# The second exchange of a spectral layer: a read fetches what one back step wrote, into a quarter of the partitions

## The chip, the cores and the metric

The kernel runs on one core of a Trainium2 chip. Its time is the device time of one execution in microseconds (us); before the change the median of three executions was 1404.33 us (1404.03 to 1405.24). The engines are named as in the profile: PE is TensorE (PEld its weight loads), DVE is VectorE, ACT is ScalarE, POOL is GpSimd, SP is SyncE, which computes nothing and issues transfers. SPq and ACTq are the instruction queues of SP and ScalarE where they issue a transfer.

## The reference, cut to what matters

Input x is 2,048 rows of 512 numbers. Four layers follow each other, each added to x: spectral, attention, spectral, attention.

```python
def _A_ref(x, w_r, w_i):                      # spectral layer
    X = jnp.fft.rfft2(x.astype(jnp.float32), axes=(-2, -1))
    X = X * (w_r + 1j * w_i)
    return jnp.fft.irfft2(X, s=(S, D), axes=(-2, -1)).astype(jnp.bfloat16)

x = x + _A_ref(_layernorm(x), A_w_r, A_w_i)
x = x + _B_ref(_layernorm(x), B_wq, B_wk, B_wv, B_wo)   # attention, 32 heads, one shared key and value head
x = x + _A_ref(_layernorm(x), A_w_r, A_w_i)
x = x + _B_ref(_layernorm(x), B_wq, B_wk, B_wv, B_wo)
```

The change touches the spectral layer alone, which runs twice. In the text "layer 0" and "layer 1" are its two runs.

## The kernel before, in words

The two-dimensional Fourier transform is done with matmuls. A transform over the 2,048 rows is split in two factors, 16 and 128, and between the factors the data has to change its layout over the partitions. This is done through DRAM: a tile is written out and read back with another arrangement. There is one such exchange on the way forward (tiles A1, D1, A2; the profile calls the SBUF tiles A and the DRAM tile D) and a second one on the way back (B1, D2, B2; the profile calls them B and D). The 256 frequencies are handled as two halves, h = 0 and 1, of 128 complex frequencies, so a row of one half is 256 numbers, 512 bytes in bf16.

The steps of a layer:

- `forward` and `first` turn rows into frequencies and do the 128-point factor. Each `first` writes two of the 16 row groups t to D1 (line 281). `cross1(g, h)` (line 284) reads a quarter of D1 back into 32 partitions of A2: `A2[32 * g:32 * g + 32, h, :, :]`.
- `filtered(j)`, j = 0 to 7: the half is h = j // 4, and b4 = 4 * (j % 4) says which four of the 16 values of b it handles. It does the 16-point factor (TensorE, line 213 in helper `rotate`), evicts (ScalarE, line 330), and multiplies by the weights (VectorE, lines 334 to 347).
- `back(j)`: the 16-point factor in the other direction, for the same four b, two at a time. Each two are evicted to B1 (line 358, once line 356) and then written to D2 (line 359): two writes of 128 KB for each `back`.
- `cross2(h, g, eng)` (line 362): reads four of the 16 t of half h into all 128 partitions of B2. Each of these reads needs all of b, so all four `back` steps of the half.
- `along(q, h)` (line 384): the 128-point factor, matmuls with table CS over the partitions of B2 for two of the 16 t, evicted to AT (lines 387 and 389).
- `last(t, h)` (lines 396 to 399): the transform back along a row, accumulated over both halves in one PSUM bank.

Four engines, PE, ACT, DVE and SP, run these steps in the order in which the program issues them (a manual schedule). The string STEPS writes out the order of the middle part: f is `filtered`, b is `back`, j empties the list of products, and x is the second exchange of half 0, all four reads of it, issued on SP after `b3`. The four reads of half 1 come later, behind all of half 0's `along`, two on SP and two on ScalarE's queue. Then come the loads of wq and wo (layer 0), the first four `last`, and the loop over half 1.

Waits are by semaphore, and an engine that waits holds up everything behind it in its queue. For SP that means that a read waiting for the landing of a write holds up every later write.

Half 0's `along` begins right after the last `back`; half 1's `along` follows the four early `last` steps.

Of the kernel before, what the change touches and what calls it, by code (L numbers as in the profile page):

```python
# [11 lines left out]
P = 128  # L12
BF = mybir.dt.bfloat16
# [32 lines left out]
VCELLS = 128  # L46
LASTW = 6
NEGATE = 7
STEPS = "f0 f1 f2 b0 f3 b1 b2 j3 b3 x0 f4 f5 f6 b4 f7 b5 j7 b6 b7"
NORMED, NORMG = (1,), ((3,), (3,), (3,))  # L50
OUTK, LATE_AT = 2, 4
TWICE = ((7,), 8)
# [23 lines left out]
def host_tables():  # L76
    import ml_dtypes
    bf = lambda a: np.ascontiguousarray(np.asarray(a, dtype=np.float32).astype(ml_dtypes.bfloat16))
    tabs = {}
    p = np.arange(P, dtype=np.float64)  # L80
    m = np.arange(P, dtype=np.float64)
    t16 = np.arange(16, dtype=np.float64)

    row = (128 * np.arange(4)[None, :, None] + np.arange(P)[:, None, None]).astype(np.float64)
    ff = (np.arange(256)[None, None, :] + 1).astype(np.float64)

    half = 2 * np.pi * np.arange(256) / 512.0
    cos, sin = np.cos(half), np.sin(half)
    cos[128], sin[0] = 0.0, 0.0
    cos[129:], sin[129:] = -cos[1:128][::-1], sin[1:128][::-1]  # L90
    turn = (row * ff).astype(np.int64) % 512
    c, s = np.concatenate([cos, -cos])[turn], -np.concatenate([sin, -sin])[turn]
    tabs["PH"] = bf(np.concatenate([c[..., :128], s[..., :128], c[..., 128:], s[..., 128:]], axis=2))

    ang = 2 * np.pi * (16 * p[:, None, None] + t16[None, :, None]) * m[None, None, :] / 2048.0
    tabs["C1"], tabs["S1"] = bf(np.cos(ang)), bf(np.sin(ang))

    ti, ai = np.divmod(np.arange(P), 8)
    same = (ai[:, None] == ai[None, :]).astype(np.float64)
    ang = 2 * np.pi * ti[:, None] * ti[None, :] / 16.0  # L100
    tabs["G"] = bf(np.stack([same * np.cos(ang), same * np.sin(ang), -same * np.sin(ang)], axis=1))

    b16 = np.arange(16, dtype=np.float64)
    mm = 16 * ai[None, None, :] + b16[None, :, None]
    ang = 2 * np.pi * (ti[:, None, None] * ti[None, None, :] / 16.0 + ti[None, None, :] * mm / 2048.0)
    tabs["H1"] = bf(same[:, None, :] * np.cos(ang))
    tabs["H2"] = bf(same[:, None, :] * np.sin(ang))

    ang = 2 * np.pi * m[:, None] * p[None, :] / 128.0
    tabs["CS"] = bf(np.stack([np.concatenate([np.cos(ang), np.sin(ang)], axis=1),  # L110
                              np.concatenate([-np.sin(ang), np.cos(ang)], axis=1)], axis=1))

    frow = (128 * np.arange(2)[None, :, None] + np.arange(P)[:, None, None] + 1).astype(np.float64)
    dd = np.arange(512)[None, None, :].astype(np.float64)
    ang = 2 * np.pi * frow * dd / 512.0
    cf = np.where(frow == 256, 1.0, 2.0) / (S * D)
    tabs["PSC"] = bf(cf * np.cos(ang))
    tabs["PSS"] = bf(-cf * np.sin(ang))
    tabs["ident"] = bf(np.eye(P, dtype=np.float32))
    tabs["hmask"] = (np.arange(P)[:, None] // DH % 2 == np.arange(2)[None, :]).astype(np.float32)  # L120
    return tabs


class Tables:


    def __init__(self, nc):
        self.nc, self.host, self.dram = nc, host_tables(), {}
# [82 lines left out]
def rotate(nc, ps, c, s, sn, re_im, first):  # L211

    nc.tensor.matmul(ps, lhsT=c, rhs=re_im, start=True, stop=False, skip_group_check=True)  # L213
    nc.tensor.matmul(ps[:, 0:128], lhsT=s, rhs=re_im[:, 128:256], start=False, stop=False, skip_group_check=True)
    nc.tensor.matmul(ps[:, 128:256], lhsT=sn, rhs=re_im[:, 0:128], start=False, stop=True, skip_group_check=True)  # L215


def spectral_layer(nc, tc, tabs, ht, A_w_r, A_w_i, x_sb, bigp, pre, norm, att, feed, weights):
    C1, S1, S1N, PH, ident = (tabs[n] for n in ("C1", "S1", "S1N", "PH", "ident"))
    with tc.tile_pool(name="workA", bufs=2) as work, tc.tile_pool(name="tabA", bufs=1) as tabA, \  # L220
# [32 lines left out]
            weights(k)  # L253

        D1 = dram.tile([2, 16, P, 256], BF, name="D1")
        D2 = dram.tile([2, P, 16, 256], BF, name="D2")
        turned = len(feed.xT)
        xT = feed.xT[0] if turned else bigp.tile([P, NC, 16, P], BF, name="xT", tag="big")
        Pk, A1, A2 = big("Pk"), big("A1"), big("A2")
# [58 lines left out]
        Z, B1, B2 = big("Z"), big("B1"), big("B2")  # L318
        M = big("M").rearrange("p h t c -> p (h t c)").rearrange("p (i j b r f) -> p i j b r f", i=2, j=4, b=4, r=2)

        def filtered(j):

            h, b4 = j // 4, 4 * (j % 4)
            hf = slice(128 * h, 128 * h + 128)
            X = work.tile([P, 4, 2, 128], BF, name="X", tag="X", bufs=3)
            for b in range(b4, b4 + 4, 2):
                ps = bank()
                for i in range(2):
                    rotate(nc, ps[:, i, :], G[:, 0, :], G[:, 1, :], G[:, 2, :], A2[:, h, b + i, :], i == 0)
                nc.scalar.copy(out=X[:, b - b4:b - b4 + 2, :, :], in_=ps.rearrange("p j (r f) -> p j r f", r=2))  # L330
            m1, m2 = (M[:, i, j % 4] for i in range(2))
            wrb = wr_sb[:, b4:b4 + 4, hf].unsqueeze(2).to_broadcast([P, 4, 2, 128])
            wib = wi_sb[:, b4:b4 + 4, hf].unsqueeze(2).to_broadcast([P, 4, 2, 128])
            nc.vector.tensor_tensor(out=m1, in0=X, in1=wrb, op=ALU.mult)
            joined()
            nc.vector.tensor_tensor(out=m2, in0=X, in1=wib, op=ALU.mult)
            products.append((j, m1, m2))
# [3 lines left out]
        def joined():  # L341

            while products:
                j, m1, m2 = products.pop()
                Zv = Z[:, j // 4, 4 * (j % 4):4 * (j % 4) + 4, :].rearrange("p b (r f) -> p b r f", r=2)
                nc.vector.tensor_tensor(out=Zv[:, :, 0, :], in0=m1[:, :, 0, :], in1=m2[:, :, 1, :], op=ALU.subtract)
                nc.vector.tensor_tensor(out=Zv[:, :, 1, :], in0=m1[:, :, 1, :], in1=m2[:, :, 0, :], op=ALU.add)  # L347

        def back(j):
            h, b4 = j // 4, 4 * (j % 4)  # L350
            for b in range(b4, b4 + 4, 2):
                ps = bank()
                for i in range(2):
                    rotate(nc, ps[:, i, :], H1[:, b + i, :], H2N[:, b + i, :], H2[:, b + i, :], Z[:, h, b + i, :], i == 0)
                if j == 7 and b > b4:
                    nc.vector.tensor_copy(out=B1[:, h, b:b + 2, :], in_=ps)
                else:
                    nc.scalar.copy(out=B1[:, h, b:b + 2, :], in_=ps)
                nc.sync.dma_start(out=D2[h, :, b:b + 2, :], in_=B1[:, h, b:b + 2, :])

        def cross2(h, g, eng):
            eng.dma_start(out=B2[:, h, 4 * g:4 * g + 4, :],
                          in_=D2[h].rearrange("(t a) b c -> t (a b) c", t=16)[4 * g:4 * g + 4].rearrange("t m c -> m t c"))

        for step in STEPS.split():
            j = int(step[1])
            if step[0] == "f":
                filtered(j)
            elif step[0] == "b":
                back(j)  # L370
            elif step[0] == "j":
                joined()
            else:
                for g in range(4):
                    cross2(0, g, nc.sync)

        AT = big("AT").rearrange("p h t c -> p (h t c)").rearrange("p (t h c) -> p t h c", t=16, h=2)

        def along(q, h, use_scalar):

            ps = bank()
            for i in range(2):
                for j in range(2):
                    nc.tensor.matmul(ps[:, i, :], lhsT=B2[:, h, 2 * q + i, 128 * j:128 * j + 128], rhs=CS[:, j, :],
                                     start=(j == 0), stop=(j == 1), skip_group_check=True)
            if use_scalar:
                nc.scalar.copy(out=AT[:, 2 * q:2 * q + 2, h, :], in_=ps)
            else:
                nc.vector.tensor_copy(out=AT[:, 2 * q:2 * q + 2, h, :], in_=ps)
# [10 lines left out]

        for q in range(8):
            along(q, 0, q % 2 == 0)
        for g in range(4):
            cross2(1, g, (nc.sync, nc.scalar)[g % 2])
        weights(20)
        early = 4
        for t in range(early):
# [2 lines left out]
        for q in range(9):  # L410
# [9 lines left out]
            g, odd = divmod(q - 3, 2)  # L420
# [746 lines left out]
def full_kernel(ctx, tc, A_x, A_w_r, A_w_i, B_x, B_wq, B_wk, B_wv, B_wo, out):  # L1167
# [63 lines left out]
    for layer in range(2):  # L1231
        norm_in, norm_out = make_norm(), make_norm()
        spectral_layer(nc, tc, tabs, ht, A_w_r, A_w_i, x_sb, bigp, norm, norm_in, att, feed,
                       weights if layer == 0 else lambda k: None)
        feed = attention_layer(nc, tc, att, norm_in, norm_out, x_sb, wo_sb, None if layer == 0 else store)
        norm = norm_out
# [47 lines left out]
```

## Time and profile before

| | us |
|---|---|
| median of three executions | 1404.33 |
| the profiled execution, its own time | 1406.89 |
| its span, first to last instruction | 1405.1 |
| granted TensorE clock over the span | 0.999 |
| spectral layer 1, first `forward` to last `last`, about | 708 to 788 |
| wait of TensorE before half 1's `along`, layer 0 | 1.87 |
| the same, layer 1 | 0.85 |

The page gives busy times and shares for each engine, the DMA queues, the chain of work that ended last, and the costliest groups of instructions by line. A timeline row has start, length, engine, line, operation and tiles, and in brackets the idle time ahead of it with what ended it. For a DMA the length in a queue's timeline is the time to issue it, and the DMA view gives the time from issue to landing; landing times in the text are the sum of the two. The text calls the eight reads of the second exchange x0 to x7 and the two writes of `back(j)` wja and wjb.

### The profile page before, as it was taken

How to read it: one execution, taken by the hardware profiler on the slowest of the kernel's cores; microseconds unless marked ns; L12 is line 12 of the kernel's file. 1: busy time of each engine (PE TensorE's matmuls, PEld its weight loads, DVE VectorE, ACT ScalarE, POOL GpSimd, SP SyncE). 2: the span in 40 equal slices, each digit the busy share in tenths (PEclk: the TensorE clock that was granted, in tenths of full speed). 3: DMA queues.
4: the chain of work that ended last, by engine and by line, in shares of the span. 5: the costliest groups of instructions: out<-in, count | busy, mean ns of one | idle time of the engine just before them, and what ended most of it. 6: DMA issues, size and time to landing. Idle time of an engine off the chain costs nothing.

```text
span 1405.1 us, 34816 instructions
## 1 busy us (share of the span) xinstructions
PE 1341.5 (95%) x14050; PEld 470.6 (33%) x14118; DVE 1310.0 (93%) x2271; ACT 1330.8 (95%) x1542; POOL 822.7 (59%) x479
## 2 busy tenths in 40 slices
PE   8799999999999999999997999999999999999998
PEld 6553232223222222222275422322222222222222
DVE  5679999999999999999966899999999999999997
ACT  6579999999999999999966899999999999999997
POOL 1125676667666667666700267666666666666664
PEclk9999999999999999999999999999999999999999
DMA  8710000000000000001074000000000000000000
GB/s 251 201 38 2 1 2 2 2 1 2 2 2 1 2 2 1 2 1 35 13 199 133 2 2 2 2 2 9 5 6 1 6 9 5 2 2 9 9 2 16
DMA packets 45682, 34.52 MB, mean 25 GB/s; under 512 B 10064, under 2 KB 43088, under 8 KB 45008
## 3 DMA queue, kind: packets, MB, share of 16 engines
q1 hardware_dynamic: 43120, 31.08, 7.8%
q8 instruction: 110, 1.80, 0.5%
q10 hardware_dynamic: 2400, 1.21, 0.3%
q14 instruction: 52, 0.43, 0.1%
HBM read 20.22 MB, written 10.49 MB: 22 GB/s over the span
## 4 chain that ended last, share of the span: by engine, by line
ACT 48%; PE 33%; issue 9%; DVE 7%; DMA 3%; SPq 0%; POOL 0%; DVEq 0%; ACTq 0%
ACT e L1082 47%; PE pv L871 13%; PE sc L916 10%; DVE ph L956 3%; PE aux L916 2%; PE ps L266 2%; DVE ln_stats L156 1%; PE aux L455 1%; PE ps L213 1%; DMA B<-D 1%; DVE ph L988 1%; PE pv L886 1%; PE aux L684 1%; DMA x_sb<-in_A_x_dram 0%; DMA D<-B 0%
## 5 line engine op out<-in xcount | busy, mean ns | idle before, releaser
L1082 ACT ACTIVATE e<-sc 128x1024 bf16<-128x1024 f32 x1328 | 1218.1, 1167 | 2.9 <-PE sc L916 2.9
L980 POOL TENSOR_TENSOR ph<-ph,step 128x1024 int32<-128x1024 int32 x404 | 762.8, 1891 | 413.1 <-DVE ph L988 292.7
L956 DVE TENSOR_SCALAR ph<-aux 128x512 uint16<-128x512 f32 x1440 | 903.8, 678 | 20.5 <-PE aux L916 15.9
L871 PE MATMUL pv<-ph,vaug 128*32 128x512 bf16 x4320 | 548.8, 386 | 0.6 <-POOL ph L980 0.3
L916 PE MATMUL sc<-QT,Kv 32*128 32x512 bf16 x2656 | 521.8, 380 | 23.5 <-ACT e L1082 16.3
L871 PE MATMUL pv<-e,vaug 128*32 128x512 bf16 x2656 | 484.0, 384 | 0.3 <-ACT e L1082 0.3
L916 PE MATMUL aux<-QT,Kv 32*128 32x512 bf16 x1440 | 455.8, 384 | 1.0 <-DVE ph L956 0.5
L916 PEld LDWEIGHTS <-Kv 32*128 32x128 bf16 x4096 | 183.4, 91 | 525.9 <-issue 517.5
L886 PE MATMUL pv<-wo_sb,zeros 128*32 128x512 bf16 x1200 | 257.8, 383 | 0.0
L871 PEld LDWEIGHTS <-vaug 128*32 128x32 bf16 x6976 | 147.5, 94 | 292.6 <-issue 281.6
L988 DVE TENSOR_SCALAR ph<-ph 128x2048 uint16<-128x2048 uint16 x316 | 216.4, 685 | 0.5
L162 POOL TENSOR_TENSOR ln_rstd<-ln_veps,mhalf 128x4 f32<-128x4 f32 x16 | 16.5, 1033 | 120.6 <-DVE ln_veps L161 120.5
L156 DVE BATCH_NORM_STATS2 ln_stats<-x_sb 128x6 f32<-128x512 bf16 x64 | 43.5, 679 | 22.9 <-ACT x_sb L418 17.0
L886 PEld LDWEIGHTS <-zeros 128*32 128x32 bf16 x1200 | 60.1, 94 | 1.9 <-issue 0.3
L786 DVE STREAM_TRANSPOSE oT<-pv 128x512 f32<-128x512 f32 x64 | 45.2, 706 | 9.2 <-PE pv L871 9.2
L185 ACT ACTIVATE Pk<-ps,ln_rstd 128x256 bf16<-128x256 f32 x64 | 26.8, 472 | 19.7 <-PE ps L266 15.2
L266 PE MATMUL ps<-tab_PH,xT 128*128 128x256 bf16 x256 | 35.3, 286 | 1.6 <-DVE oT L786 0.8
L280 DVE CAST A<-ps 128x512 bf16<-128x512 f32 x28 | 19.3, 689 | 18.3 <-PE ps L215 18.3
L455 PE MATMUL aux<-xTa,wq_sb 128*128 128x512 bf16 x90 | 32.6, 384 | 2.8 <-issue 2.4
L808 POOL TENSOR_TENSOR on<-oT,rden 128x512 bf16<-128x512 f32 x30 | 31.7, 1056 | 2.0 <-DVE rden L812 1.8
L684 PE MATMUL aux<-wo_sb,ph 128*128 128x512 bf16 x72 | 26.1, 383 | 3.6 <-issue 2.1
L213 PE MATMUL ps<-Z,tab_H 128*128 128x256 bf16 x64 | 15.1, 275 | 13.0 <-DVE Z L347 12.9
(108 smaller groups left out, 669.7 us busy)
## 6 DMA issues: line engine op xcount, KB each, us to landing
D<-A SPq DMA_DIRECT2D x32, 128.0 KB, 2.9
A<-D SPq DMA_DIRECT2D x16, 256.0 KB, 3.5
D<-B SPq DMA_DIRECT2D x32, 128.0 KB, 2.4
B<-D SPq DMA_DIRECT2D x12, 256.0 KB, 4.0
wr_sb<-in_A_w_r_dram SPq DMA_DIRECT2D x2, 1024.0 KB, 6.2
wi_sb<-in_A_w_i_dram SPq DMA_DIRECT2D x2, 1024.0 KB, 8.5
tab_H<-const_H SPq DMA_DIRECT2D x4, 512.0 KB, 6.8
out_dram<-x_sb SPq DMA_DIRECT2D x15, 128.0 KB, 1.7
```

The lines of the kernel that those rows point to most:

```text
L156: nc.vector.bn_stats(st, src)
L266: nc.tensor.matmul(ps[:, j, :], lhsT=xT[:, cc, 2 * k + j, :], rhs=PH[:, cc, 256 * h:256 * h + 256], start=(cc == 0), stop=(cc == NC - 1), ...
L455: self.nc.tensor.matmul(ps, lhsT=w(c), rhs=self.xTq[:, c, qc * 512:(qc + 1) * 512], start=(c == 0), stop=(c == NC - 1), skip_group_check=True)
L684: nc.tensor.matmul(ps, lhsT=OTs[qb][:, g4, kk * P:(kk + 1) * P], rhs=wo_sb[:, g4, :], start=first, stop=last, skip_group_check=True)
L786: end = clock.now(clock.FLIP, lambda: nc.vector.transpose(out=oT[:, par].rearrange("p b c -> p (b c)"), in_=pv), clock.last + clock.MM_END)
L871: nc.tensor.matmul(pv_tiles[gi][32 * i:32 * i + 32, :], lhsT=vaug[:, kc, j, :], rhs=es, start=((gi, i) not in started), stop=(left[gi, i] ...
L886: nc.tensor.matmul(pv_tiles[gi][32 * i:32 * i + 32, :], lhsT=att.zeros, rhs=wo_sb[:, 0, :], start=False, stop=False, skip_group_check=True)
L916: nc.tensor.matmul(out, lhsT=Kv[r, par, kc * P:(kc + 1) * P], rhs=QT[r, g, qb * 512:(qb + 1) * 512], start=True, stop=True, skip_group_che ...
L956: end = clock.now(clock.Z, lambda: nc.vector.tensor_scalar(out=z.bitcast(U16), in0=ps, scalar1=SCALE * LOG2E * 128.0, scalar2=127.0 * 128. ...
L980: nc.gpsimd.tensor_tensor(out=copy.bitcast(I32), in0=z.bitcast(I32), in1=step.to_broadcast([P, w // 2]), op=ALU.add)
L988: nc.vector.tensor_scalar(out=one.bitcast(U16), in0=z.bitcast(U16), scalar1=float(PHASE[1]), scalar2=None, op0=ALU.add)
L1082: nc.scalar.activation(out=e[:, 0:ng * 512], in_=sc[:, 0:ng, :].rearrange("p a b -> p (a b)"), func=ACT.Exp, scale=SCALE)
```

## The change

A read of the second exchange now fetches the block that one `back` step has written. D2 is arranged by that step, `[half, step, partition, 4 b, 256]`, and the block's 32 values of m go into 32 partitions of B2, with all 16 t. So a read depends on two writes and not on eight, and there is one read behind each `back`: STEPS now lists all eight, x0 to x7, and all are issued on SP. The 128 values of m then lie in B2's partitions in another order, and the rows of table CS, over which `along` sums, are put in that order on the host. Sizes stay: a read is 256 KB in rows of 512 bytes, a write 128 KB with 1,024 bytes of each partition.

```diff
-STEPS = "f0 f1 f2 b0 f3 b1 b2 j3 b3 x0 f4 f5 f6 b4 f7 b5 j7 b6 b7"
+STEPS = "f0 f1 f2 b0 f3 b1 x0 b2 x1 j3 b3 x2 x3 f4 f5 f6 b4 f7 b5 x4 j7 b6 x5 b7 x6 x7"
...
     tabs["CS"] = bf(np.stack([np.concatenate([np.cos(ang), np.sin(ang)], axis=1),
-                              np.concatenate([-np.sin(ang), np.cos(ang)], axis=1)], axis=1))
+                              np.concatenate([-np.sin(ang), np.cos(ang)], axis=1)], axis=1)[16 * (np.arange(P) // 4 % 8) + 4 * (np.arange(P) // 32) + np.arange(P) % 4])
...
-        D2 = dram.tile([2, P, 16, 256], BF, name="D2")
+        D2 = dram.tile([2, 4, P, 4, 256], BF, name="D2")
...
-                nc.sync.dma_start(out=D2[h, :, b:b + 2, :], in_=B1[:, h, b:b + 2, :])
-
-        def cross2(h, g, eng):
-            eng.dma_start(out=B2[:, h, 4 * g:4 * g + 4, :],
-                          in_=D2[h].rearrange("(t a) b c -> t (a b) c", t=16)[4 * g:4 * g + 4].rearrange("t m c -> m t c"))
+                nc.sync.dma_start(out=D2[h, j % 4, :, b - b4:b - b4 + 2, :], in_=B1[:, h, b:b + 2, :])
+
+        def cross2(h, g):
+            nc.sync.dma_start(out=B2[32 * g:32 * g + 32, h, :, :],
+                              in_=D2[h, g].rearrange("(t a) b c -> t (a b) c", t=16).rearrange("t m c -> m t c"))
...
             else:
-                for g in range(4):
-                    cross2(0, g, nc.sync)
+                cross2(j // 4, j % 4)
...
         for q in range(8):
             along(q, 0, q % 2 == 0)
-        for g in range(4):
-            cross2(1, g, (nc.sync, nc.scalar)[g % 2])
         weights(20)
```

## The prediction

> **What bounds the kernel now.** I read the page first, for the busy shares and the chain that ended last, then that chain inside the two spectral stages, then what TensorE waited for there, then SP's queue and the landing of each transfer. The page:
>
> ```profile
> span 1405.1 us, 34816 instructions
> ...
> PE 1341.5 (95%) x14050; PEld 470.6 (33%) x14118; DVE 1310.0 (93%) x2271; ACT 1330.8 (95%) x1542; POOL 822.7 (59%) x479
> ...
> ACT 48%; PE 33%; issue 9%; DVE 7%; DMA 3%; SPq 0%; POOL 0%; DVEq 0%; ACTq 0%
> ...
> A<-D SPq DMA_DIRECT2D x16, 256.0 KB, 3.5
> D<-B SPq DMA_DIRECT2D x32, 128.0 KB, 2.4
> B<-D SPq DMA_DIRECT2D x12, 256.0 KB, 4.0
> ```
>
> Three engines are busy 93 to 95% of the span and DMA is only 3% of the chain; that 3% lies in the spectral stages, which are what the change touches. The chain there, layer 0 and then layer 1 (start, length, what):
>
> ```profile
> 62.99 3.17 DMA D<-B
> ...
> 66.28 3.41 DMA B<-D
> ...
> 69.74 0.62 PE ps L384 x4
> ...
> 757.72 2.07 DMA D<-B
> ...
> 760.07 3.34 DMA B<-D
> ...
> 763.46 0.62 PE ps L384 x4
> ```
>
> In both layers the last write of `back(7)` lands (66.16; 759.79), the first read of half 1 is issued and lands (69.69; 763.41), and `along(0, 1)` starts. TensorE's timeline shows how much of that is uncovered:
>
> ```profile
> 69.74 1.05 PE L384 MATMUL ps<-tab_CS,B 128*128 128x256 bf16 x8 [1.87 <-DMA B<-D]
> ...
> 763.46 1.05 PE L384 MATMUL ps<-tab_CS,B 128*128 128x256 bf16 x8 [0.85 <-DMA B<-D]
> ```
>
> TensorE idles 1.87 and 0.85 us; before that it has work of its own (half 0's `along` and four `last`). **So the second exchange can give back at most 1.87 + 0.85 = 2.72 us**, 0.19% of the time: an earlier landing meets TensorE still busy until 67.87 and 762.61.
>
> **The change part by part.**
>
> *Table CS permuted, D2 reshaped:* the same bytes in the same 128 KB load (4.3 us, landing at 50.7, needed at 61.62), the same matmul shapes, the same 1,024 contiguous bytes per partition in each write. Nothing; if CS landed late, 11 us of cover would go first.
>
> *Two reads per layer leave ScalarE's queue:* their issue takes 1.0 us (66.30 to 67.31; 760.10 to 761.09), inside ScalarE's idle 4.92 and 3.90 us before line 387. Nothing. SP issues eight reads instead of six.
>
> *The first gate of half 1:* before, `along(0, 1)` needs one read (four t, all partitions) of the four issued together. After, it needs all of x4 to x7, each with 16 t for 32 partitions, but only x7 must wait for `back(7)`'s last write. The other three reads of before land behind the gate (layer 0: 70.20 and 71.30 for two) and TensorE waited for none, so no more is won there.
>
> *The reads' new places in SP's queue.* SP issues in order, and a read waits there until the writes that it fetches have landed; behind it stand the writes of the next back steps. Prices for this, one DMA at a time from the DMA view: issues follow 0.48 us apart (744.42, 744.90). A write alone lands after 1.9 to 2.0 us (742.22 to 746.30). A read into 32 partitions of 256 KB is the first exchange's A<-D: 3.2, 3.3, 3.2, 3.4 us in layer 1 (issued 733.78, 731.17, 736.29, 737.70), 3.2 to 3.5 in layer 0 where the tables are not in flight, 4.5 and 5.9 where they are. A write issued behind such a read lands 0.15 us after it (read 734.47, write 734.60; read 736.98, write 737.13).
>
> The new read itself is not in the trace. Its lower end is the first of four B<-D reads, with the same 512-byte rows but 128 partitions: 2.7 and 2.8 us (56.66, 748.31). Its upper end is 4.5 (A<-D of layer 0, issued 46.06). A<-D has its 32 partitions but rows of 8 KB. I take 3.3, since the destination is the same quarter. [...]
>
> Layer 0, with w4b for the second write of `back(4)`. SP comes to D<-B only at 50.23, after the tables:
>
> ```profile
> 49.63 0.51 SPq L1204 DMA_DIRECT2D wv_sb<-in_B_wv_dram  x1
> 50.23 4.30 SPq L359 DMA_DIRECT2D D<-B  x8
> 56.66 2.03 SPq L362 DMA_DIRECT2D B<-D  x4
> 58.73 4.58 SPq L359 DMA_DIRECT2D D<-B  x8
> 66.28 0.92 SPq L362 DMA_DIRECT2D B<-D  x2
> ```
>
> The reader sees eight writes back to back, a wait, four reads, eight writes. After: w0b lands 53.14, x0 issues 53.2, lands 56.5. w2b issues 54.2, lands 56.7 behind x0. x1 issues 54.7, lands 58.0; w3b 55.6, lands 58.2; x2 waits for w2b, 56.8; x3 waits for w3b, 58.3, lands 61.6. w4a and w4b 58.8 and 59.2 (before: 58.73 on), landing 61.8 behind x3; w5b 60.2, lands 62.2. x4 waits for w4b, 61.9, lands 65.2. Behind it w6a and w6b, ready at 61.05, issue at 62.4 and 62.9 and land at 65.4; x5 63.3, lands 66.6; w7a and w7b 63.8 and 64.3 (before 62.25 and 62.99), landing 66.8 behind x5 (before 66.16, 3.2 us behind four reads). x6 65.5; x7 66.9, lands 70.2. Against 69.69: **+0.5 us**. x3's 61.6 just meets half 0's `along` at 61.62; were it later, the later gate would cover it.
>
> Layer 1, where no tables stand ahead and writes are issued as they come: x0 to x3 issue by 748.5, ahead of w4a at 751.18. w4b lands 753.7; x4 issues 754.1 behind w5b, lands 757.4. w6b 755.82, lands 757.8. x5 756.3, lands 759.6; w7b 757.3, lands 759.8 behind it (before 759.79). x7 issues 760.0, lands 763.3 against 763.41: **-0.1 us**.
>
> **Sum** +0.5 - 0.1 = +0.4 us. The profiled execution took 1406.89 us (span 1405.1 and 1.8 around it), 2.56 above the median of 1404.33; the shift adds to either, and after both gates the same instructions follow in the same order. Against the median: 1404.33 + 0.4 = **1404.7 us**.
>
> How it leans on the read's price: in layer 0 x1, x3, x4, x5 and x7 each stand behind a write that stood behind the read before, so 0.1 us per read moves x7 by about 0.4; in layer 1 by 0.17. At 2.7 us x7 lands at or before TensorE's floor in both layers: -2.7 us, 1401.6. At 3.7: +2.3 and +0.7, 1407.3. At 4.5: +5.1 and +2.2, 1411.6.
>
> **The rivals.**
>
> *Short reads.* If the 512-byte rows set the price, 2.7 to 3.0 us: 1401.6 to 1403.0. For it: the B<-D rows above; against: every 32-partition row, 3.2 at least. 17%.
>
> *Reads that block SP (the other side).* SP's order of reads ahead of later writes, in layer 0's second half, turns each slow read into a late write; above 3.65 us a read the time is over 0.2% longer, at 4.5 it is 1411.6. For it: A<-D's median is 3.5 and two of layer 0's took 4.5 and 5.9; x4, w6, x5 and w7 come as close together as those. Against: the tables that stood beside those two are gone by 52.6. 25%, 20% of it past 0.2%.
>
> *The gate closes too early.* x4 to x7 are now written ahead of half 0's `along` in program order. If its dependence covered all of B2, TensorE would do its 6.2 us of half 0's work (61.62 to 67.87; 756.36 to 762.61) only after x7: +6.7 and +6.1 us, 1417.1. Against it: `filtered(0)` reads A2 half 0 at 39.86 though A2's half 1 was not yet fetched, its last quarter landing only at 50.56, and line 213 waited for that with half 1:
>
> ```profile
> 50.59 0.28 PE L213 MATMUL ps<-A,tab_G 128*128 128x256 bf16 x1 [0.26 <-DMA A<-D]
> ```
>
> Likewise a read of D1 was issued at 731.17 while a write to other rows of D1 (730.69) landed only at 732.49, so a read does not wait for foreign blocks. 3%.
>
> *Nothing but jitter in SP's issues:* some of them took 0.82 and 1.31 us (756.79, 740.75) with no cause in view; such a one ahead of x7 adds up to 1 us. 5%, inside 0.2%.
>
> **How the numbers follow.** My case (3.1 to 3.6 us a read) has 50%: 1403.6 to 1406.7. About 0.2% (2.8 us) is what a measurement of this kernel can tell from no change. A gain past it is above the 2.72 us that TensorE idles, so it needs something I do not see: 5%, taken from the short reads. Slower: 20% from slow reads, 3% from the gate, 2% from my own case with both layers late. Within: 70%. The range is 1402.4 to 1408.5: it leaves out the shortest of the short reads (8%), the slow reads past 3.9 us (9%) and the gate (3%).
>
> **What would show it.** Right: D<-B and B<-D alternate in SP's queue; a read lands in 3.1 to 3.6 us; the idle before line 384's half 1 is about 2.4 us in layer 0 and 0.7 in layer 1; x5 is issued ahead of w7a in both; ScalarE issues no B<-D. Wrong: a read under 3.0 us and an idle near zero; or w7b issued after 65 us in layer 0; or line 384's first matmul itself waiting for DMA.

## The result and the profile after

The changed kernel takes 1412.05 us (median of four executions, 1411.15 to 1414.47), the kernel before, on the same chip, 1404.78 us (1404.03 to 1405.36). The ratio is 1.0055, with a 95% interval of 1.0043 to 1.0067. The change costs 7.3 us; the forecast was +0.4. Of the four executions the two with a lower mean granted clock (0.995 and 0.996 instead of 0.999) are the longer ones, by 1.7 and 3.3 us, and the reason for that turns out to be part of the result.

The page of the changed kernel (span; busy time of the engines; the shares of the chain; the transfers of the second exchange with KB and median time to landing):

```profile
span 1409.4 us, 34882 instructions
...
PE 1353.1 (96%) x14118; PEld 471.0 (33%) x14118; DVE 1310.4 (93%) x2271; ACT 1331.1 (94%) x1542; POOL 821.1 (58%) x479
...
ACT 47%; PE 36%; issue 8%; DVE 6%; DMA 1%; POOL 0%; SPq 0%; DVEq 0%; ACTq 0%
...
D<-B SPq DMA_DIRECT2D x32, 128.0 KB, 2.8
B<-D SPq DMA_DIRECT2D x16, 256.0 KB, 3.3
```

VectorE and ScalarE do what they did, within 0.4 us. TensorE's 11.6 us more are not all longer work: the profile before has only 14,050 records of its matmuls and this one 14,118, with 14,118 weight loads in both. The reads have become shorter (median 3.3 us instead of 4.0) and all 16 are on SP; the writes have become longer (2.8 instead of 2.4). The chain at the gate of half 1, layer 0 and then layer 1 (start, length, what):

```profile
64.81 3.14 DMA D<-B
...
68.01 3.19 DMA B<-D
...
71.44 1.38 PE ps L383 x8
...
761.61 3.04 DMA D<-B
...
764.72 2.95 DMA B<-D
...
767.72 0.62 PE ps L383 x4
```

The form is that of before: last write of `back(7)`, a read, `along(0, 1)`. To see what got longer, each gate is measured from the same event, the end of `back(7)`'s last eviction (VectorE, line 356), after which nothing but transfers stands between the data and the gate:

| us | before, layer 0 | after, layer 0 | before, layer 1 | after, layer 1 |
|---|---|---|---|---|
| last eviction ends | 62.51 | 61.06 | 757.25 | 760.52 |
| until its write is issued (the hold) | 0.48 | 3.75 | 0.47 | 1.09 |
| write, issue to landing | 3.17 | 3.14 | 2.07 | 3.04 |
| read that the gate needs last | 3.41 | 3.19 | 3.34 | 2.95 |
| last eviction to start of `along(0, 1)` | 7.23 | 10.38 | 6.21 | 7.20 |
| TensorE idle there | 1.87 | 4.29 | 0.85 | 1.84 |

So the new read that the gate waits for is no slower than the old one, and the gates come 3.15 and 0.99 us later all the same: in layer 0 because SP issues the last write 3.3 us later, in layer 1 because it is issued 0.6 later and lands 1.0 later. SP's queue of the changed kernel in layer 0 (start, time to issue, line):

```profile
61.52 0.32 SPq L362 DMA_DIRECT2D B<-D  x1
61.89 1.80 SPq L359 DMA_DIRECT2D D<-B  x2
63.80 0.37 SPq L362 DMA_DIRECT2D B<-D  x1
64.22 1.01 SPq L359 DMA_DIRECT2D D<-B  x2
65.71 2.62 SPq L362 DMA_DIRECT2D B<-D  x2
```

Reads and writes alternate. x4 stands at the head until w4b has landed (61.50). Then SP needs 3.3 us to issue x4, w6a, w6b, x5 and w7a, while w7b has been ready since 61.06; it goes out at 64.81. One of these issues, that of w6b, took 1.23 us alone.

TensorE's timeline at the gate of layer 0 shows a second cost:

```profile
71.44 1.38 PE L383 MATMUL ps<-tab_CS,B 128*128 128x256 bf16 x8 [4.29 <-DMA B<-D]
72.72 0.61 PE L397 MATMUL ps<-tab_PSC,AT 128*128 128x512 bf16 x1
...
75.76 0.38 PE L397 MATMUL ps<-tab_PSC,AT 128*128 128x512 bf16 x1
```

The same eight matmuls took 1.05 us before, and a matmul of 128x512 takes 0.61 us here and 0.38 a few us later. The profile in the stretches between the changes of the granted clock says why (columns: stretch and its length; busy time and count of PE, PEld, DVE, ACT, POOL; granted clock; DMA share; GB/s):

```profile
68.57:71.98 3.41, 0.54 (x5) 0.52 (x6) 0.00 (x0) 0.00 (x0) 0.00 (x0) 1.00 0.87 253
71.98:75.40 3.42, 3.42 (x14) 1.64 (x12) 0.95 (x3) 2.34 (x4) 0.00 (x0) 0.50 0.41 131
```

TensorE was busy for 0.54 us of one stretch of 3.41 us, and the next stretch runs at half clock; the one after that, from 75.40 on, has its full clock again. The kernel before has no such stretch but one that begins 1.5 us before its end. With that the two profiles add up. Each row says how much later than before the changed kernel is at that point, and the last column what the stretch ahead of it added:

| point | before | after | later by | added |
|---|---|---|---|---|
| last eviction, layer 0 | 62.51 | 61.06 | -1.45 | -1.45 |
| gate, layer 0 | 69.74 | 71.44 | +1.70 | +3.15 |
| last eviction, layer 1 | 757.25 | 760.52 | +3.27 | +1.57 |
| gate, layer 1 | 763.46 | 767.72 | +4.26 | +0.99 |
| end of the span | 1405.1 | 1409.4 | +4.3 | 0.0 |

The first row is not counted: kernels with the same work up to that point (two further below) reach it at 60.84 and 62.09. The other rows are the change: 3.15 and 0.99 us at the gates and 1.57 us between them, together 5.7. The profiled executions lie 4.3 us apart (1406.89 and 1411.2) and the medians 7.3, because the one of before is 2.1 above its median and the one of after 0.85 below. Of the 7.3 the profiles thus account for 5.7; the rest is taken up again under the clock.

### The profile page after: what moved, and what is told of

Read it like the earlier page. It is cut to its first block, busy times and chain, and to the rows that moved or that the text cites. A ratio compares the mean times of both kernels' runs of the same rounds, so it can differ in the third digit from the quotient of the medians.

```text
span 1409.4 us, 34882 instructions
## 1 busy us (share of the span) xinstructions
PE 1353.1 (96%) x14118; PEld 471.0 (33%) x14118; DVE 1310.4 (93%) x2271; ACT 1331.1 (94%) x1542; POOL 821.1 (58%) x479
## 4 chain that ended last, share of the span: by engine, by line
ACT 47%; PE 36%; issue 8%; DVE 6%; DMA 1%; POOL 0%; SPq 0%; DVEq 0%; ACTq 0%
ACT e L1079 46%; PE pv L868 14%; PE sc L913 11%; DVE ph L953 2%; PE aux L913 2%; PE ps L266 2%; PE aux L452 1%; PE ps L213 1%; DVE ln_stats L156 1%; PE aux L681 1%; PE pv L883 1%; DVE ph L985 1%; PE ps L383 1%; PE ps L397 1%; PE ps L398 1%
## 5 line engine op out<-in xcount | busy, mean ns | idle before, releaser
L452 PE MATMUL aux<-xTa,wq_sb 128*128 128x512 bf16 x120 | 39.5, 385 | 0.4 <-DVE ph L953 0.2
L681 PE MATMUL aux<-wo_sb,ph 128*128 128x512 bf16 x96 | 31.8, 384 | 1.5 <-DVE ph L953 1.0
L386 ACT CAST AT<-ps 128x512 bf16<-128x512 f32 x24 | 14.1, 592 | 15.7 <-PE ps L383 14.4
```

The lines of the kernel that those rows point to most:

```text
L452: self.nc.tensor.matmul(ps, lhsT=w(c), rhs=self.xTq[:, c, qc * 512:(qc + 1) * 512], start=(c == 0), stop=(c == NC - 1), skip_group_check=True)
L681: nc.tensor.matmul(ps, lhsT=OTs[qb][:, g4, kk * P:(kk + 1) * P], rhs=wo_sb[:, g4, :], start=first, stop=last, skip_group_check=True)
```

## The experiments

After the result three causes stood against each other. **Q**: SP's queue, a read that waits or is issued ahead of a write holds that write. **C**: traffic, the data of the quarter reads delay the writes that run beside them. **K**: the clock, TensorE's idle time at the gate has grown long enough to bring the granted clock down. Against all three stood a fourth, that the layout alone does it: a gate that needs four reads instead of one.

### Where the reads stand in SP's queue

All four kernels keep the new layout and change only the place of the reads (`layout_alone` also the queue of two of them).

`layout_alone` puts the reads where the kernel before has them: half 0's behind `b3`, half 1's behind half 0's `along`, on SP and ScalarE in turn.

```diff
-STEPS = "f0 f1 f2 b0 f3 b1 x0 b2 x1 j3 b3 x2 x3 f4 f5 f6 b4 f7 b5 x4 j7 b6 x5 b7 x6 x7"
+STEPS = "f0 f1 f2 b0 f3 b1 b2 j3 b3 x0 x1 x2 x3 f4 f5 f6 b4 f7 b5 j7 b6 b7"
...
-        def cross2(h, g):
-            nc.sync.dma_start(out=B2[32 * g:32 * g + 32, h, :, :],
+        def cross2(h, g, eng=nc.sync):
+            eng.dma_start(out=B2[32 * g:32 * g + 32, h, :, :],
...
         for q in range(8):
             along(q, 0, q % 2 == 0)
+        for g in range(4):
+            cross2(1, g, (nc.sync, nc.scalar)[g % 2])
```

> Edit: the new layout and table, but every read at the place and on the queue of the kernel before (half 0 behind b3 on SP, half 1 behind half 0's along, on SP and ScalarE's queue in turn). Along of half 1 now needs all four quarters where before it needed the first read. If the four quarters land like the four reads of before (layer 0: 69.69, 70.20, 71.30 and later), the gate is 2 to 2.5 us later in each layer: idle about 4 and 3 us, time 1409 to 1411. If quarter-partition reads were slower as such: 1413 or more. If they were as fast and the gate did not matter: 1405.

1413.04 us, ratio 1.0053 [1.0039, 1.0067]. `reads_behind_b7` keeps all reads on SP and moves x4 and x5 behind `b7`:

```diff
-STEPS = "f0 f1 f2 b0 f3 b1 x0 b2 x1 j3 b3 x2 x3 f4 f5 f6 b4 f7 b5 x4 j7 b6 x5 b7 x6 x7"
+STEPS = "f0 f1 f2 b0 f3 b1 x0 b2 x1 j3 b3 x2 x3 f4 f5 f6 b4 f7 b5 j7 b6 b7 x4 x5 x6 x7"
```

> Edit: half 1's reads x4 to x7 are issued behind back(7)'s writes, half 0's as in the changed kernel. Theory Q (SP's order: a read that waits for its writes holds up the writes behind it): the second write of back(7) is issued within 0.6 us of its eviction in both layers (changed kernel: 3.75 us in layer 0, 1.1 us in layer 1) and lands within 2.6 us; the four reads then stand close together at about 1.2 us each, so half 1's along starts 2 to 3 us earlier in layer 0 and about as in the changed kernel in layer 1, TensorE's idle in layer 0 falls under 2 us; time about 1407. Theory C (the 32-partition reads slow the writes wherever they stand): the four stacked reads cost more than they gain, 1412 or more.

1413.39 us, ratio 1.0052 [1.0038, 1.0066]. TensorE's timeline of `reads_behind_b7` at the gates of both layers, and SP's queue of it in layer 0:

```profile
70.59 1.86 PE L383 MATMUL ps<-tab_CS,B 128*128 128x256 bf16 x8 [3.37 <-DMA B<-D]
...
768.61 1.28 PE L383 MATMUL ps<-tab_CS,B 128*128 128x256 bf16 x8 [2.50 <-DMA B<-D]
```

```profile
59.95 2.26 SPq L359 DMA_DIRECT2D D<-B  x4
62.30 2.41 SPq L362 DMA_DIRECT2D B<-D  x4
```

The hold is gone: the last write is issued 0.03 us after its eviction, in both layers, so Q is right that what stands ahead of it on SP holds it (not all of that is reads: the last section has an issue that took 0.8 us longer than the others). It lands after 2.4 and 1.8 us. But the time does not get better, because the gate now needs four reads issued together: their landings in layer 0 are 66.3, 67.6, 69.1 and 70.5, 1.3 to 1.5 us apart, and the gate comes 8.73 and 7.85 us after the last eviction, where the kernel before needed 7.23 and 6.21. **That is the price of the layout with the hold gone, 1.5 and 1.6 us**: of the old four reads the gate needed only the first, of the new ones all. In `layout_alone` it is 11.51 and 7.88 us; in its layer 0 the two reads on ScalarE's queue went out at 64.18 and 64.66, with the loads of wq and wo beside them, and took 6.3 and 7.7 us. Its layer 1, without these loads, is the same as `reads_behind_b7`.

`reads_one_step_later` puts one more `back` between a write and the read that waits for it; `half0_as_before` takes half 0's reads out of the stretch and leaves half 1's as the change has them:

```diff
-STEPS = "f0 f1 f2 b0 f3 b1 x0 b2 x1 j3 b3 x2 x3 f4 f5 f6 b4 f7 b5 x4 j7 b6 x5 b7 x6 x7"
+STEPS = "f0 f1 f2 b0 f3 b1 b2 j3 b3 x0 x1 x2 x3 f4 f5 f6 b4 f7 b5 x4 j7 b6 x5 b7 x6 x7"
...
+STEPS = "f0 f1 f2 b0 f3 b1 x0 b2 x1 j3 b3 x2 x3 f4 f5 f6 b4 f7 b5 j7 b6 x4 b7 x5 x6 x7"
```

(first `half0_as_before`, then `reads_one_step_later`)

> Edit: x4 behind back(6), x5, x6, x7 behind back(7), so that no read waits for a write that has not had a whole back step to land. Theory Q: back(7)'s second write is issued at most 1.5 us after its eviction in layer 0, the gate there is about 2 us earlier than in the changed kernel; time about 1407. Theory C: no gain, 1411 to 1413.

> Edit: the changed kernel with half 0's four reads together behind b3, as before; half 1's stay between the back steps. If layer 0's late gate comes from half 0's reads holding up SP where it is already behind the tables: layer 0's along of half 1 starts 1 to 2 us earlier, layer 1 unchanged, 1409.5 to 1411. If it comes from half 1's reads alone: layer 0 no better (the four reads together also delay back(4)'s writes, 4.3 to 4.6 us of landing in the kernel before), 1411.5 to 1414.

`reads_one_step_later`: 1411.84 us, ratio 1.0044 [1.0031, 1.0058]; hold 2.14 and 0.48 us, the write lands 2.2 and 2.9 us after its issue, the last read 4.8 and 4.0 us later, gate after 9.27 and 7.50 us. `half0_as_before`: 1412.93 us, ratio 1.0049 [1.0037, 1.0062]; hold 3.31 and 1.44, gate after 10.65 and 7.54. So it is not the place of half 0's reads that holds half 1's writes; x4 and x5 do. And each place of the reads trades one wait for another: fewer reads ahead of the last write means a shorter hold and more reads behind it, each worth 1.3 to 1.5 us. None of the four orders reaches the 7.23 and 6.21 us of before.

### The clock

`tensor_kept_busy` adds twelve matmuls, whose result nobody reads, between the four early `last` steps and half 1's `along`:

```diff
             last(t, 0)
+        ps = psum.tile([P, 512], F32, name="ps", tag="pa")
+        for _ in range(12):
+            nc.tensor.matmul(ps, lhsT=ident, rhs=PSC[:, 0, :], start=True, stop=True, skip_group_check=True)
```

> Edit: the changed kernel with 12 more matmuls of no use ahead of half 1's along (2.6 us of TensorE's idle filled). Theory K (an idle of about 4 us makes the clock granted to TensorE fall to half for 3.4 us after it): layer 0's idle falls from 4.3 to about 1.7 us, no half-clock stretch follows line 383 in layer 0, its matmuls there are 0.22 us apart and not 0.43, and the time falls by 1.5 to 2 us or more, to 1408.5 to 1410.5, with less spread from run to run. Rival (the slow matmuls have another cause, such as the transfers of wq and wo): they stay slow, 1411 to 1412.5. In layer 1 the filling may delay the gate by up to 0.6 us.

1409.93 us, ratio 1.0037 [1.0024, 1.0049]. That interval still touches the changed kernel's (1.0043 to 1.0067), and the executions spread as before (1408.88 to 1412.74 us), so the profile has to tell them apart. The stretch ahead of its gate in layer 0 among the windows, and the gate in TensorE's timeline:

```profile
67.30:70.71 3.41, 2.51 (x12) 0.95 (x10) 0.00 (x0) 0.00 (x0) 0.00 (x0) 1.00 0.78 206
```

```profile
71.43 1.03 PE L383 MATMUL ps<-tab_CS,B 128*128 128x256 bf16 x8 [1.61 <-DMA B<-D]
```

The gate comes as late as in the changed kernel (10.16 us after the eviction), the clock stays at 1.00, and the eight matmuls take 1.03 us again. From this gate to the last eviction of layer 1 the profile has 687.76 us; the kernel before has 687.51, the changed one 689.08. So in the profiles the clock is worth 1.3 to 1.6 us in layer 0, and K is right, though not the whole: the gates stay 2.93 and 1.57 us late, which is most of the 5.0 us that are left between the medians. In layer 1 the added matmuls were themselves the last to end (766.97, x7 had landed at 765.53), so this kernel gives away up to 1.4 us there.

The same two distances, from a gate to the next point, follow the time at half clock in the other kernels too (us; distances as more than before; stretches at half clock that begin in the last 2 us of the span or behind it left out):

| kernel | at half clock, gate 0 to last eviction of layer 1 | that distance | at half clock, gate 1 to the end | that distance |
|---|---|---|---|---|
| before | 0 | 0 (687.51) | 0 | 0 (641.64) |
| before_early6 | 0 | -0.1 | 0 | -0.15 |
| before_busy | 0 | 0.0 | 0 | 0.0 |
| tensor_kept_busy | 0 | +0.25 | 0 | 0.0 |
| writes_on_act | 2.7 | +0.7 | 0 | 0.0 |
| after | 3.4 | +1.57 | 0 | 0.0 |
| reads_one_step_later | 3.4 | +1.51 | 3.4 | +1.25 |
| early_reads_small | 3.4 (and a memset) | +2.0 | 0 | 0.0 |
| half1_reads_on_pool_busy | 4.1 | +1.85 | 0 | +0.35 |
| half0_as_before | 4.2 | +1.90 | 3.4 | +1.25 |
| half1_reads_on_pool | 4.6 | +2.05 | 2.9 | +1.35 |
| writes_on_act_busy | 4.7 | +1.75 | 0 | 0.0 |
| layout_alone | 5.0 | +1.91 | 3.4 | +1.35 |
| reads_behind_b7 | 5.8 | +2.66 | 3.4 | +1.35 |

A whole stretch of 3.41 us costs 1.2 to 1.4 us in layer 1 and 1.5 to 1.6 in layer 0. The profiled execution of the changed kernel escaped layer 1's: the stretch that decides had 1.57 us of matmuls in it. Its longer executions, at a clock of 0.995 and 0.996, must have had more of it: the kernels whose profiles hold 15.5 and 10.9 us at half clock have 0.995 and 0.996 (`half1_reads_on_pool`, `layout_alone`), so these had two or three stretches more than the profiled one. That fits their extra 1.7 and 3.3 us, and the 1.6 us that the profiles leave of the difference of medians, but no trace shows those executions, so it is argued and not shown.

### The traffic

`early_reads_small` leaves the order as the change has it, but x4, x5 and x6 fetch only 2 of the 16 t; x7 is whole. A memset on VectorE fills what they leave out.

```diff
+        nc.vector.memset(B2[0:96, 1, 2:16, :], 0.0)
...
-            nc.sync.dma_start(out=B2[32 * g:32 * g + 32, h, :, :],
-                              in_=D2[h, g].rearrange("(t a) b c -> t (a b) c", t=16).rearrange("t m c -> m t c"))
+            n = 2 if h and g < 3 else 16
+            nc.sync.dma_start(out=B2[32 * g:32 * g + 32, h, 0:n, :],
+                              in_=D2[h, g].rearrange("(t a) b c -> t (a b) c", t=16)[0:n].rearrange("t m c -> m t c"))
```

> Edit: x4, x5 and x6 fetch only 2 of their 16 t (32 KB in place of 256 KB); the rest of those partitions of B2's half 1 is set to zero, so the output is not the reference's. Order and waits in SP's queue stay, the transfers nearly go. Theory C: back(7)'s second write lands in about 2 us in place of 3.0 to 3.1, its issue in layer 0 moves up by 1 us or more because the writes that the reads wait for land sooner too, gate 2 to 3 us earlier in layer 0 and about 1 us in layer 1, 1406 to 1409. Theory Q: the gate moves by under 1 us in each layer, 1410 to 1412.

Last write: hold 2.28 and 0.34 us (3.75 and 1.09 in the changed kernel), landing after 1.9 and 1.8 us (3.1 and 3.0), gate after 7.97 and 5.19 us (10.38 and 7.20). TensorE's timeline at its gates:

```profile
71.54 1.03 PE L385 MATMUL ps<-tab_CS,B 128*128 128x256 bf16 x8 [2.61 <-DMA B<-D]
...
766.26 1.05 PE L385 MATMUL ps<-tab_CS,B 128*128 128x256 bf16 x8
```

So C is right too: without their data the landing of the last write falls by 1.2 to 1.3 us, back to what a write alone takes (1.9 to 2.0 us in layer 1 of the kernel before, issued 742.22 to 746.30), and in layer 1 the gate comes 1.0 us sooner than in the kernel before and TensorE does not wait. That is what the change would bring if the early reads cost nothing. The time of this kernel, 1411.44 us, ratio 1.0037 [1.0024, 1.0050], does not show it: the memset takes 1.55 us of VectorE in each layer, the profile has a half-clock stretch at 743 us, ahead of the exchange, and from gate 0 to the last eviction of layer 1 it is 2.0 us longer than before. Its time is therefore inconclusive and its gates are what counts.

### Other queues

`writes_on_act` issues the writes of `back(6)` and `back(7)` on ScalarE, so that no read stands ahead of them; `writes_on_act_busy` is the same with five matmuls added as above.

```diff
-                nc.sync.dma_start(out=D2[h, j % 4, :, b - b4:b - b4 + 2, :], in_=B1[:, h, b:b + 2, :])
+                (nc.scalar if j >= 6 else nc.sync).dma_start(out=D2[h, j % 4, :, b - b4:b - b4 + 2, :], in_=B1[:, h, b:b + 2, :])
```

> Edit: the changed kernel with the four writes of back(6) and back(7) issued on ScalarE's queue, so that no write stands behind x4 or x5 on SP; the reads keep their places. Theory Q: back(7)'s second write is issued within 0.7 us of its eviction in both layers and lands within 2.7 us; half 1's along starts 2 to 3 us earlier than in the changed kernel in layer 0 and 1 to 1.5 us earlier in layer 1; time 1405 to 1408. Theory C (what counts is that quarter reads take 1.3 us each of the transfer engines, as the reads behind back(7) showed): the reads pile up to x7 all the same, gate earlier by under 1 us, 1410 to 1412.

> Edit: the same with 5 matmuls of no use (1.1 us) ahead of half 1's along, so that a remaining idle does not bring the clock down. Theory K: no half-clock stretch but the one at the program's end, 0.5 to 2 us under the kernel with the writes on ScalarE alone; 1404 to 1406.5. Rival: no difference.

1416.46 us, ratio 1.0079 [1.0065, 1.0092], and 1414.76 us, ratio 1.0063 [1.0050, 1.0077]. The five matmuls don't keep the clock up in layer 0: half clock runs from 72.99 to 79.82 us. The gates come 13.03 and 8.58 us after the eviction in `writes_on_act`. SP's waits and SP's queue of it in layer 0 (the wait: total, times, longest):

```profile
SPq L359 <- DMA D<-B: 2.9, 1, 2.9
```

```profile
62.35 1.86 SPq L359 DMA_DIRECT2D D<-B  x4
...
66.76 2.07 SPq L362 DMA_DIRECT2D B<-D  x4
```

A write of `back(4)`, which reads only what ScalarE had evicted, waited 2.9 us for the landing of another write, and everything on SP behind it came late, x4 at 66.76. So the edit put in a wait that the kernel did not have, and it does not tell Q from the rest. The wait is on semaphore 110, with which the write then reports its own landing, and a write that ScalarE had issued at 59.73 had used it last (landed 62.28): the two transfers share a semaphore, not data. In layer 1 the same happens to the second write of `back(5)`, issued at 763.12 behind a landing at 763.06.

`half1_reads_on_pool` issues x4 to x7 on GpSimd instead, `half1_reads_on_pool_busy` the same with five added matmuls:

```diff
-            nc.sync.dma_start(out=B2[32 * g:32 * g + 32, h, :, :],
+            (nc.gpsimd if h else nc.sync).dma_start(out=B2[32 * g:32 * g + 32, h, :, :],
```

> Edit: x4 to x7 are issued by GpSimd, which is idle there, so that no write stands behind a read in SP's queue; all data as in the changed kernel. Theory Q: back(7)'s second write is issued within 0.8 us of its eviction in both layers (3.75 and 1.1 in the changed kernel); if GpSimd's reads land in 3 to 4 us like SP's, half 1's along starts 2 to 3.5 us earlier in layer 0 and up to 1 us earlier in layer 1, 1405 to 1408. Theory C: the writes still land in 3 us behind the reads and the gate moves by less than 1.5 us in layer 0, 1410 or more. GpSimd's own cost of issuing is not in any trace yet; above 1.5 us a read it would show in x7.

> Edit: x4 to x7 on GpSimd, and 5 matmuls of no use (1.1 us) ahead of half 1's along. Theory K: where the idle that is left would bring the clock down, it no longer does: no half-clock stretch at half 1's along, 0 to 2 us under the kernel without them; rival: the same time or 0.5 us more.

1418.35 us, ratio 1.0089 [1.0075, 1.0103], and 1416.05 us, ratio 1.0071 [1.0057, 1.0085]. TensorE's gate in layer 0 of `half1_reads_on_pool`:

```profile
74.38 1.86 PE L383 MATMUL ps<-tab_CS,B 128*128 128x256 bf16 x8 [7.97 <-DMA B<-D]
```

In layer 0 the hold is gone again (0.03 us; 0.41 in layer 1), and what comes in its place is that SP, free of the reads, sends out the loads of wq and wo at 61.45 and 63.04, ahead of the last reads: these then take up to 9.5 us. In layer 1, which has no such loads, the gate is still later (8.43 us) than in the changed kernel (7.20). In SP's queue the reads had also held back 1 MB of loads. With the five matmuls the half clock of layer 1 is gone, that of layer 0 is not (74.34 to 81.17 us).

### Cover for the idle time of the kernel before

Two kernels leave the change out and fill the 1.87 us of the kernel before: `before_early6` does six `last` steps ahead of half 1's `along`, `before_busy` adds four matmuls.

```diff
-        early = 4
+        early = 6
```

> Edit: the kernel before the change with six early steps last(t, 0) in place of four, so that 1.3 us of TensorE's own later work fills its idle of 1.87 and 0.85 us. If the idle can be filled with work that is on the path afterwards: 1 to 2 us faster, 1402.5 to 1404. If what follows the gate is bound by evictions and layer-norm on the other engines: no change, or 0.5 us slower in layer 1, where the work is longer than the idle.

> Edit: the kernel before the change with 4 matmuls of no use (0.86 us) at the same place. Theory K, carried to the kernel before: its idle of 1.87 us in layer 0 brings the clock down in some executions (its times fall into groups near 1404 and 1406.8) and not in others; with the idle at 1.0 us it never does, so the upper group goes and the median falls by 0 to 1 us, to about 1404.2. Rival: the two groups have another cause and stay.

1405.89 us, ratio 0.9997 [0.9988, 1.0006], and 1405.16 us, ratio 0.9994 [0.9985, 1.0002]. TensorE's idle time in layer 0 falls to 0.76 and 0.62 us and nothing is gained: the gate is set by transfers, and the kernel before had no half-clock stretch there to lose. Neither kernel can be told from the one before by its median. One sign speaks for the expectation of `before_busy`: none of its 11 executions is above 1406.13 us, and 10 of the 21 of the kernel before are. But five of those ten had a mean clock of 0.999 or more, so what makes the longer ones stays open.

## Why the prediction was wrong

The range was 1402.4 to 1408.5 and the time is 1412.05 against a forecast of 1404.7. Most of the chance (70%) was put on no change, and the kernel is slower. By the prediction's own steps:

- **What bounds the kernel, and the most that can be won (2.72 us of idle time): right.** In layer 1 of `early_reads_small`, where the early reads cost nearly nothing, TensorE's idle time vanishes and nothing more.
- **The read's price, 3.3 us: right.** 3.19 and 2.95 for the reads that the gate waits for, 3.3 in the median of 16, 11 of them within 3.1 to 3.6; the longest, x4 of layer 1, took 4.53. Short reads were excluded by that.
- **Layer 0, "w7a and w7b 63.8 and 64.3", 1.8 us after w7b is ready at 62.51: the step that failed.** Measured: 3.75 us. x4 was to go out 0.6 us before the last eviction and went out 0.46 after it, 1.06 of the difference. That comes from half 0: from SP's first write to the landing of w4b the forecast has 11.6 us (50.23 to 61.8), and it took 12.7 (48.81 to 61.5), 0.6 of these 1.1 us in later landings of w3b and w4b behind reads (next point), the rest in issues. The other 0.9 lies behind x4, most of it in w6b's issue of 1.23 us.
- **"A write issued behind such a read lands 0.15 us after it": mis-sized.** It is 0.2 to 0.6 us for the first of two writes and 0.45 to 0.75 (once 1.4) for the second, which the forecast counts on. The forecast gives the last write 2.5 us from issue to landing in both layers (64.3 to 66.8; 757.3 to 759.8); it took 3.14 and 3.04. `early_reads_small` shows the reads' data as the cause.
- **Layer 1, w7b issued at 757.3, 0.05 us after its eviction: mis-sized.** 1.09 us; ahead of it stood the issues of x5 (0.37 us) and w7a, behind a w6b that took 1.12 us to issue. Here it is this long issue more than the reads: in `tensor_kept_busy`, same order and no long issue of w6 in layer 1, the hold is 0.27 us and x7 lands 6.36 us after the last eviction (7.15 in the changed kernel; 6.16 for the first read before). The prediction had such issues (0.82 and 1.31 us with no cause in view) as a rival of 5% that stays within 0.2%; alone it does.
- **The sum.** From last eviction to gate the forecast has 7.7 and 6.1 us, measured are 10.38 and 7.20, together 3.8 us more. The half clock, **a term that the prediction does not have**, is 1.57 more. 0.4 + 3.8 + 1.6 = 5.8, against the 5.7 of the table above. The prediction gave 2.4 us as the idle time of layer 0 that would show it right; it never asked what a longer one does to TensorE's clock. The profile of before had nothing of it but a stretch that begins 1.5 us before the end.
- **The rivals.** "Reads that block SP" named the mechanism, the place (layer 0's second half) and, at its upper price, the time, 1411.6 us. It had 25%, because it was tied to slow reads: the writes are held by reads of normal length, since each issue and each landing ahead of them counts. "The gate closes too early" fell: half 0's `along` starts at 60.91 and 759.63, ahead of the landings of x4 to x7. Layer 0's start lies 0.09 us behind the landing of x3 (60.82) after 0.58 us of idle time (the eviction that the timeline names had ended at 60.52), so there it probably waited for x3, a sign that the prediction gave for being wrong; the later gate covers it, as the prediction said of a later x3.
- **Why a new read takes 3.3 us: not shown.** The forecast took 3.3 from the first exchange's reads into 32 partitions (3.2 to 3.4 us in layer 1 of the kernel before), whose rows are 8 KB; no run ahead of the forecast shows a read into 32 partitions in rows of 512 bytes, and the changed kernel has 3.3 in the median of 16. That the quarter of the partitions is the reason is not shown by this, since no read into 128 partitions ran alone. Four reads issued together, layer 1, kernel before and then `layout_alone` (windows; the last column is GB/s):

```profile
761.11:765.01 3.90, 2.81 (x17) 1.34 (x16) 0.00 (x0) 0.91 (x2) 0.00 (x0) 1.00 0.99 269
```

```profile
763.72:769.17 5.45, 3.51 (x21) 1.75 (x18) 1.38 (x2) 0.82 (x2) 0.00 (x0) 1.00 1.03 192
```

The same 1 MB takes 5.45 us instead of 3.90, at 0.71 of the rate, and the median packet of 512 bytes takes 42 ns instead of 27. Both stretches begin slowly; in their middle (764.70 to 769.00 and 762.30 to 764.70) it is 189 GB/s against 323, 0.59 of the rate. In a single new read of the changed kernel the median packet takes 27 ns as well.

## What to carry to other kernels

A read split by who wrote its data can start earlier, but then the consumer needs every part: count the landing of the last part, not of the first, and price the parts stacked (1.3 to 1.5 us each here). In a queue that issues in order, a read placed ahead of a later write is a wait put in front of that write (in layer 0 the last write went out 3.75 us after its eviction, and 0.03 us after it with x4 and x5 behind `b7`); reckon its hold from the moment the write is ready, with every issue that stands ahead of it. And when a change lengthens an idle time of TensorE, ask whether the clock survives it: here 1.87 us did, 4.29 us did not, and it cost 1.6 us on top of a delay of 3.15.

## What the runs showed of the hardware

**In these profiles the granted clock changed on a grid of 3.41 us, and what counted was the busy time within one stretch of it.** In the changed kernel it falls at 71.98, rises at 75.40 and falls again at 1410.01, behind its last instruction and 391 stretches of 3.413 us after the rise. The windows of the stretch that decides and of the one that follows, for `reads_one_step_later` and then `writes_on_act`:

```profile
763.54:766.95 3.41, 1.27 (x7) 0.50 (x6) 0.00 (x0) 0.00 (x0) 0.00 (x0) 1.00 0.60 103
766.95:770.37 3.42, 3.42 (x14) 1.66 (x13) 0.40 (x1) 1.92 (x4) 0.00 (x0) 0.50 0.00 0
```

```profile
766.82:770.23 3.41, 1.44 (x7) 0.48 (x5) 0.00 (x0) 0.00 (x0) 0.00 (x0) 1.00 1.20 191
770.23:773.65 3.42, 1.92 (x13) 1.11 (x13) 0.00 (x0) 1.31 (x3) 0.00 (x0) 1.00 0.03 3
```

After 1.27 us of matmuls in a stretch the next one is at half clock, after 1.44 us it is not. The busiest stretch at full clock that was followed by half clock had 1.38 us (`writes_on_act_busy`, 69.58 to 72.99); counted over all 14 profiles, from the first record of the clock on (17.8 us into the span of the kernel before, 17.4 in the changed one), none of the 32 stretches at full clock before a half clock is busier than 1.38 us, 40% of the stretch, and none of the 5,644 others at full clock is less busy than 1.44 (1.66 in the kernel before, 1.57 in the changed one). At half clock 1.62 us did not end it (`layout_alone`, 70.66 to 74.07, followed by another such stretch), 3.42 us did (changed kernel, 71.98 to 75.40). So the same idle time can pass or fail by where it lies on the grid: 2.14 us in layer 1 of `reads_one_step_later` brought the clock down, 3.23 us in layer 1 of `writes_on_act` did not.

**Issue times on SP.** Most issues follow each other after 0.4 to 0.6 us (0.37 to 0.58 in layer 0 of the changed kernel), but that of w6b took 1.23 and 1.12 us in the changed kernel, and in layer 0 of every kernel with x4 ahead of a write on SP one of the writes behind x4 took 1.2 to 2.1. The DMA view of 62.36 to 63.70, where the first of them lies, has among its queues:

```profile
q8 instruction: 1, 0.02, 4.5%
```

This is a transfer of 16 KB on the instruction queue, which ended at 63.32; the issue ended 0.37 us later. Of the 28 issues on SP for the second exchange that took over 0.8 us, in all 14 profiles, 25 end 0.37 to 0.41 us behind such a transfer (4 of the 5 in the kernel before and the changed one, 0.37 to 0.39). That the transfer is the cause is not shown: no view names the engine that its instructions are for, and no experiment moved it. In layer 0 of the kernel before the transfer ran from 62.96 to 63.92, when SP issued nothing after w7b. In the changed kernel the long issue of w6b stands for about 0.8 us of the hold in layer 0 and 0.7 in layer 1, an estimate from its 1.23 and 1.12 us against the 0.45 of the others.
